# Retention attention, gated MoE and tanh MoE on one core: state products as four 64x64 tiles over two PSUM banks, block loads in two parts per batch on one queue

## The chip, the cores and the metric

The kernel runs on one core of one Trainium2 chip. The metric is device time in microseconds (us) of one execution; the time of a kernel is the median of several runs. The profile and the trace come from one further, profiled execution.

## The reference

Eight batches of eight heads with 576 positions of 64 numbers each go through retention attention; the result, 4608 tokens by 512, goes through a gated MoE and then a second MoE:

```python
scores = (q @ k.T) / sqrt(64)                      # per batch and head, 576 x 576
x   = (scores * gamma[h] ** (i - j) where i >= j, else 0) @ v
a, b = x @ w1, x @ w2                              # 512 -> 1024
y   = ((a * b) @ w3) @ w_out                       # 1024 -> 1024 -> 512
h   = y @ w2_in                                    # 512 -> 2048
out = (h - tanh(h)) @ w2_out                       # 2048 -> 512
```

## The kernel before, in words

**Dense products.** Every dense operand is split into a high and a low fp32r part, and `mm3` (L121, L122, L123) makes three matmuls of one product. Tokens go in 12 tiles of T = 384. The first stretch of the program is a loop over 96 **units**, a unit being one token tile and one of the eight 128-wide blocks of w1 and w2: `half_s` makes a = x w1 into one PSUM bank (psab), `finish` evicts the unit before (ScalarE copies a at L426, VectorE multiplies it by b out of the second bank at L428 into the tile pf), `half_s` makes b. The products pf leave for DRAM (pdr) on the queue of SyncE (SP) at the next unit's start: `later` holds the store, `tick` issues it (L116). The four banks of the pool psm serve psab and psw (the products of a fold w3 w_out, whose result w34 goes to DRAM and back, L510). After the units come the y product and the second MoE, which the change does not touch.

**Attention.** Each batch is taken in five chunks of 128 positions, the last of 64. A running state of 64x64 per head carries what earlier chunks leave. Per chunk: `attn_2` multiplies k and q of each head (pss, L263) and VectorE masks the result into pt (L265); `attn_3` makes the output pso from the state (L361, chunks after the first) and from pt and v (L367), and the state's increment psu (L375), which VectorE adds (L383 in a batch's first chunk, L385 after it); `attn_x` copies pso into the x tiles as high part (ScalarE, L398) and low part (VectorE, L399). Four more PSUM banks, the pool psa, are taken in turn by psq, psk, pss, pso and psu. The state is kept as one 128x128 block per pair of heads with zeros off the diagonal, so that a state product contracts over 128 rows and gives 64 columns.

**Two ways to do chunks.** The first two batches (10 chunks) are the **prologue**: written out by hand and then by the tables `chunk_at` and `conv_at`, with transposes of q and k on TensorE (L246), while the weights w1 and w2 are loaded and split (`Conv`, L137 to L167, mostly VectorE). The other six batches (**main part**) follow the list `stages`, one chunk each 2.26 units: q and k arrive in 32x32-blocked form (`load_qk` queues up small DMAs, 32 KB each; `trickle`, L299, issues up to TRK = 12 of them at a unit's start, in turn on SP's queue and on ScalarE's), GpSimd scales q (L328), VectorE transposes the blocks (L346, L348). `side_s` does the fold in small steps, at each unit's end; its last step loads w34 back (L510).

The order on each engine is the order in which the program is written. A DMA issue takes its place in the order of the engine that issues it, and all DMAs share eight semaphores in turn.

Of the kernel before, what the change touches and what calls it, by code (L numbers as in the profile page):

```python
# [8 lines left out]
F32 = mybir.dt.float32  # L9
# [4 lines left out]
AF = mybir.ActivationFunctionType  # L14
ALU = mybir.AluOpType
# [13 lines left out]
def retention_glu_tanh_kernel(  # L29
# [16 lines left out]
    PE, ACT, DVE, POOL, SP = nc.tensor, nc.scalar, nc.vector, nc.gpsimd, nc.sync  # L46
# [3 lines left out]
    P = 128  # L50
# [74 lines left out]
    class Conv:  # L125
# [5 lines left out]
        def load(self):  # L131
            self.pool, bufs = (hv, 4) if self.pool == "head" else (cv, 3)
            self.raw = self.pool.tile([P, 512], I64, name="raw", bufs=bufs)
            dst = self.raw
            if len(self.src.shape) == 3:
                dst = dst.rearrange("p (k m) -> p k m", k=self.src.shape[1])
            SP.dma_start(out=dst, in_=self.src)  # L137
# [65 lines left out]
    qsrc = [t.rearrange("b h s d -> b s h d") for t in (q, k, v)]  # L203
    chunks = [(b, c) for b in range(B) for c in range(NA)]
    A = {}
    state = cpool.tile([P, NP, P], F32, name="state")
    POOL.memset(state, 0.0)
    xt = {}

    def xtile(t):  # L210
# [43 lines left out]
    def attn_2(i, pool):  # L254
        b, c = chunks[i]
        s0, n = CH[c]
        kn, vn, qT, kT = A[i]
        pt = pool.tile([P, NP, 2, C], F32, name="pt")
        pss = [psa.tile([P, NP, C], F32, tag="a", name="pss") for _ in range(2)]
        for j in range(NP):  # L260
            for e in range(2):
                r = D * e
                PE.matmul(pss[e][:n, j, :n], kT[r:r + D, j, :n], qT[r:r + D, j, :n], start=True, stop=True)  # L263
        for e in range(2):
            DVE.tensor_tensor(  # L265
                pt[:n, :, e, :n], pss[e][:n, :, :n],
                mask[:n, :n].unsqueeze(1).to_broadcast([n, NP, n]), op=ALU.mult,
            )
        A[i] = (kn, vn, qT, pt)


    QK = {}
    pend = []

    def load_qk(i):

        if i >= len(chunks) or i in QK:
            return
        b, c = chunks[i]
        s0 = CH[c][0]  # L280
        e0 = min(s0 + 2 * C, S)
        m = (e0 - s0) // W
        ts = []
        for nm, src in (("q", q), ("k", k)):
            t = ap_.tile([P, NP, 2 * C // W, W], F32, name=f"{nm}b", bufs=2)
            ts.append(t)
            for r in range(P // W):
                o = t[r * W:r * W + W, :, :m]
                s_ = src[b, r // 2::2, s0:e0, (r % 2) * W:(r % 2) * W + W]
                for j in range(NP):  # L290
                    pend.append((t, o[:, j], s_[j].rearrange("(j i) c -> i j c", i=W)))
        QK[i] = ts
        if c + 1 < NA:
            QK[i + 1] = ts

    def trickle(n):
        for e in range(min(n, len(pend))):
            _, o, i_ = pend.pop(0)
            (SP, ACT)[e % 2].dma_start(out=o, in_=i_)  # L299

    def need(tile_):
        while any(e[0] is tile_ for e in pend):
            trickle(1)
# [12 lines left out]
            ts.append(t)  # L316
        KV[i] = ts

    def next_pair(i):
        return len(chunks) if i >= len(chunks) else i + (2 if chunks[i][1] + 1 < NA else 1)  # L320

    def stage_q(i):
        b, c = chunks[i]
        s0, n = CH[c]
        m, j0, k0 = n // W, s0 // W, (c % 2) * (C // W)
        need(QK[i][0])
        qn = QK[i][0][:, :, k0:k0 + m, :]
        POOL.tensor_tensor(  # L328
            qn, qn, dec_b[:, :, j0:j0 + m].unsqueeze(3).to_broadcast([P, NP, m, W]), op=ALU.mult
        )  # L330
# [7 lines left out]
    def stage_0(i):  # L338
        b, c = chunks[i]
        s0, n = CH[c]  # L340
        m, j0, k0 = n // W, s0 // W, (c % 2) * (C // W)
        qb, kb = QK.pop(i)
        need(kb)
        qn = qb[:, :, k0:k0 + m, :]
        kt = ap_.tile([P, NP, C // W, W], F32, name="kT")
        DVE.transpose(kt[:, :, :m, :], kb[:, :, k0:k0 + m, :])  # L346
        qt = ap_.tile([P, NP, C // W, W], F32, name="qT")
        DVE.transpose(qt[:, :, :m, :], qn)  # L348
        if c % 2 == 1 or c + 1 == NA:
            load_qk(next_pair(next_pair(i - c % 2)))  # L350
        A[i] = (*KV[i], qt.rearrange("p g j c -> p g (j c)"), kt.rearrange("p g j c -> p g (j c)"))

    def attn_3(i):
        b, c = chunks[i]
        s0, n = CH[c]
        kn, vn, qT, pt = A.pop(i)
        po = psa.tile([P, NP, C], F32, tag="a", name="pso")
        if c > 0:
            for j in range(NP):
                for e in range(2):  # L360
                    PE.matmul(  # L361
                        po[D * e:D * e + D, j, :n], state[:, j, D * e:D * e + D], qT[:, j, :n],
                        start=(j == 0), stop=False, skip_group_check=True,
                    )
        for j in range(NP):
            for e in range(2):
                PE.matmul(  # L367
                    po[D * e:D * e + D, j, :n], vn[:n, 2 * j + e, :], pt[:n, j, e, :n],
                    start=(c == 0 and j == 0), stop=(j == NP - 1), skip_group_check=True,
                )  # L370
        if c + 1 < NA:
            pu = psa.tile([P, NP, D], F32, tag="a", name="psu")
            for j in range(NP):
                for e in range(2):
                    PE.matmul(  # L375
                        pu[D * e:D * e + D, j, :], kn[:n, 2 * j + e, :], vn[:n, 2 * j + e, :],
                        start=True, stop=True,
                    )
            for e in range(2):
                sl = slice(D * e, D * e + D)  # L380
                st = state[sl, :, sl]
                if c == 0:
                    DVE.tensor_copy(st, pu[sl])  # L383
                else:
                    DVE.tensor_tensor(st, pu[sl], st, op=ALU.add)  # L385
        A[i] = po

    def attn_x(i):
        b, c = chunks[i]
        s0, n = CH[c]  # L390
        po = A.pop(i)
        t0 = b * S + s0
        while t0 < b * S + s0 + n:
            ti = t0 // T
            m = min((ti + 1) * T, b * S + s0 + n) - t0
            x = xtile(ti)
            a0, o0 = t0 - b * S - s0, t0 - ti * T
            ACT.activation(x[:, 0, :, o0:o0 + m], po[:, :, a0:a0 + m], AF.Copy)  # L398
            DVE.tensor_tensor(  # L399
                x[:, 1, :, o0:o0 + m], po[:, :, a0:a0 + m], x[:, 0, :, o0:o0 + m].bitcast(F32), op=ALU.subtract  # L400
            )
            t0 += m


# [15 lines left out]
    def finish():  # L420

        if not open_:
            return
        t, m, pss = open_.pop()
        a = tp.tile([P, T], F32, name="a", bufs=1)
        ACT.activation(a, pss[0][:, :T], AF.Copy)  # L426
        pf = tp.tile([P, T], F32, name="pf", bufs=3)
        DVE.tensor_tensor(pf, a, pss[1][:, :T], op=ALU.mult)  # L428
        later(SP, pdr[t][:, m], pf, 1)
        if m == FF - 1:  # L430
            del xt[t]


    def w12_target(m, i):
        def f(j):
            if i == 0:
                ws[m] = slot(m, f"w12_{m}")
            j.high = ws[m][:, i * 1024:i * 1024 + 512]
            j.low = ws[m][:, i * 1024 + 512:i * 1024 + 1024]
        return f  # L440

    q12 = Queue([
        Conv((w1, w2)[i][:, m * P:m * P + P].rearrange("(k p) c -> p k c", p=P), target=w12_target(m, i), pool="head")
        for m in range(FF) for i in range(2)
    ], ahead=3)
    wo = {}
# [114 lines left out]
    NH = 2 * NA  # L561
    J = q12.jobs
    warm = cpool.tile([P, 1], F32, name="warm")
    ACT.activation(warm, state[:, 0, 0:1], AF.Copy)
    attn_load(0)
    attn_load(1)
    J[0].load()
# [61 lines left out]
        stages += [(p - 1, stage_q, (i,)), (p, stage_0, (i,)), (p + 1, stage_1, (i,)), (p + 2, attn_4, (i,))]  # L629
    stages.sort(key=lambda e: e[0])  # L630

    TRK = 12
    NO = 84
    side_n = {}
    sn = 0
# [6 lines left out]
    for n, (t, m) in enumerate(units):  # L642
# [8 lines left out]
        if n == NO:  # L651
# [3 lines left out]
            lp[0] = lp_.enter_context(tc.tile_pool(name="lp", bufs=2, side="right", reuse_waits="tile"))  # L655
            side, sn = side_o(), 0
        n0, n1, steps = (N0, NO - 1, 79) if n < NO else (NO, len(units) - 3, 18)
        tick()
        trickle(TRK)
        i = chunk_at.get(n)  # L660
# [26 lines left out]
            scale_v(4)  # L687
            scale_q(5)
        if n == 10:
            load_qk(NH)  # L690
            load_kv(NH)
        if n == 13:
            load_qk(next_pair(NH))
        if n == len(units) - 5:
            for e in range(3):
                p_load(e)
# [4 lines left out]
        while si < len(stages) and stages[si][0] <= n:  # L701
            stages[si][1](*stages[si][2])
            si += 1
        while side is not None and sn < (n - n0 + 1) * steps / (n1 - n0):
            sn += 1
            if next(side, 1) == 1:
                side = None
# [205 lines left out]
```

## Time and profile before

| | us |
|---|---|
| three runs, median (lowest to highest) | 1647.47 (1646.09 to 1649.54) |
| profiled execution, its own time | 1644.21 |
| its span, first to last instruction | 1642.4 |
| TensorE busy in the span | 1603.5 (98%) |
| VectorE, ScalarE, GpSimd busy | 1121.9, 871.4, 30.6 |

The profiled execution lies 3.3 us below the median of the runs. The units run from 27 us to 638 us, the prologue's chunks until 106 us, and those of the main part until 580 us.

### The profile page before, as it was taken

How to read it: one execution, taken by the hardware profiler on the slowest of the kernel's cores; microseconds unless marked ns; L12 is line 12 of the kernel's file. 1: busy time of each engine (PE TensorE's matmuls, PEld its weight loads, DVE VectorE, ACT ScalarE, POOL GpSimd, SP SyncE). 2: the span in 40 equal slices, each digit the busy share in tenths (PEclk: the TensorE clock that was granted, in tenths of full speed). 3: DMA queues.
4: the chain of work that ended last, by engine and by line, in shares of the span. 5: the costliest groups of instructions: out<-in, count | busy, mean ns of one | idle time of the engine just before them, and what ended most of it. 6: DMA issues, size and time to landing. Idle time of an engine off the chain costs nothing.

```text
span 1642.4 us, 26856 instructions
## 1 busy us (share of the span) xinstructions
PE 1603.5 (98%) x10128; PEld 1492.8 (91%) x10128; DVE 1121.9 (68%) x2006; ACT 871.4 (53%) x1930; POOL 30.6 (2%) x35
## 2 busy tenths in 40 slices
PE   7899899999998999999999999999999999999999
PEld 6899889999898999999999999999999999999998
DVE  6964665455543357666658778778787877877876
ACT  5533333222322223444367777677767777777766
POOL 0000101010100000000000000000000000000000
PEclk9999999999999999999999999999999999999999
DMA  9646757465547257766540010001000000001000
GB/s 230 165 100 147 151 141 160 123 144 129 118 107 202 65 178 259 225 200 209 193 161 20 20 39 20 20 20 39 20 20 20 26 33 20 20 20 40 1 20 20
DMA packets 261250, 157.96 MB, mean 96 GB/s; under 512 B 209152, under 2 KB 238080, under 8 KB 261120
## 3 DMA queue, kind: packets, MB, share of 16 engines
q1 hardware_dynamic: 199488, 139.71, 30.3%
q10 hardware_dynamic: 61632, 16.53, 4.3%
q8 instruction: 79, 1.29, 0.3%
q14 instruction: 51, 0.42, 0.1%
HBM read 110.05 MB, written 46.14 MB: 95 GB/s over the span
## 4 chain that ended last, share of the span: by engine, by line
PE 86%; DMA 6%; DVE 5%; SPq 1%; ACT 1%; ACTq 1%; issue 1%; DVEq 0%
PE psh L123 8%; PE psh L122 8%; PE psh L121 8%; PE psout L122 8%; PE psout L121 8%; PE psout L123 8%; PE psab L121 6%; PE psab L123 6%; PE psab L122 6%; PE psy L121 4%; PE psy L123 4%; PE psy L122 4%; DMA pdr<-pf 2%; DMA qb<-in_q_dram 2%; PE pso L367 1%; DMA kb<-in_k_dram 1%
## 5 line engine op out<-in xcount | busy, mean ns | idle before, releaser
L121 PE MATMUL psab<-x,w 128*128 128x384 f32 x768 | 265.4, 346 | 15.3 <-ACT a L426 15.2
L123 PE MATMUL psh<-yhl,w2i 128*128 128x384 f32 x768 | 258.9, 337 | 0.0
L123 PE MATMUL psab<-x,w 128*128 128x384 f32 x768 | 258.5, 337 | 0.3 <-DVE x L399 0.3
L122 PE MATMUL psab<-x,w 128*128 128x384 f32 x768 | 258.4, 336 | 0.0
L121 PE MATMUL psh<-yhl,w2i 128*128 128x384 f32 x768 | 258.4, 336 | 0.0
L122 PE MATMUL psh<-yhl,w2i 128*128 128x384 f32 x768 | 258.3, 336 | 0.0
L122 PE MATMUL psout<-w2o,g 128*128 128x512 f32 x576 | 226.8, 394 | 0.0
L121 PE MATMUL psout<-w2o,g 128*128 128x512 f32 x576 | 225.9, 392 | 0.0
L123 PE MATMUL psout<-w2o,g 128*128 128x512 f32 x576 | 225.5, 391 | 0.0
L802 ACT ACTIVATE u<-psh 128x384 f32<-128x384 f32 x192 | 94.5, 492 | 221.5 <-PE psh L123 221.2
L121 PEld LDWEIGHTS psab<-x,w 128*128 128x128 f32 x768 | 145.3, 189 | 21.6 <-ACT a L426 17.9
L810 DVE TENSOR_TENSOR w<-u,psh 128x384 f32<-128x384 f32 x192 | 106.1, 553 | 80.8 <-ACT th L804 80.6
L823 DVE TENSOR_TENSOR g<-w,g 128x384 fp32r<-128x384 f32 x192 | 107.1, 558 | 69.1 <-ACT g L822 69.0
L121 PEld LDWEIGHTS psh<-yhl,w2i 128*128 128x128 f32 x768 | 144.2, 188 | 8.0
L122 PEld LDWEIGHTS psh<-yhl,w2i 128*128 128x128 f32 x768 | 144.1, 188 | 7.4
L426 ACT ACTIVATE a<-psab 128x384 f32<-128x384 f32 x96 | 46.8, 487 | 190.5 <-DMA qb<-in_q_dram 85.7
L123 PEld LDWEIGHTS psab<-x,w 128*128 128x128 f32 x768 | 145.3, 189 | 0.6 <-DVE x L399 0.6
L122 PEld LDWEIGHTS psab<-x,w 128*128 128x128 f32 x768 | 145.4, 189 | 0.3
L123 PEld LDWEIGHTS psh<-yhl,w2i 128*128 128x128 f32 x768 | 144.0, 187 | 0.0
L817 DVE COPY_PREDICATED w<-u,th 128x384 f32<-128x384 int32 x192 | 116.5, 607 | 20.9 <-DVE w L816 0.9
L123 PEld LDWEIGHTS psout<-w2o,g 128*128 128x128 f32 x576 | 108.3, 188 | 24.0
L121 PE MATMUL psy<-p,w 128*128 128x384 f32 x384 | 128.3, 334 | 0.0
(86 smaller groups left out, 2832.6 us busy)
## 6 DMA issues: line engine op xcount, KB each, us to landing
pdr<-pf SPq DMA_DIRECT2D x96, 192.0 KB, 3.0
pin<-pdr SPq DMA_DIRECT2D x48, 384.0 KB, 4.2
raw<-in_moe_w_dram SPq DMA_DIRECT2D x32, 512.0 KB, 4.7
raw<-in_moe_w_out_dram SPq DMA_DIRECT2D x24, 512.0 KB, 4.4
ydr<-ys ACTq DMA_DIRECT2D x12, 768.0 KB, 5.7
yin<-ydr SPq DMA_DIRECT2D x12, 768.0 KB, 4.3
out_dram<-os SPq DMA_DIRECT2D x36, 256.0 KB, 2.2
kn<-in_k_dram SPq DMA_DIRECT2D x32, 256.0 KB, 3.6
```

Source lines behind the costliest of these rows:

```text
L121: PE.matmul(ps, lh, rh, start=first, stop=False)
L122: PE.matmul(ps, ll, rh, start=False, stop=False)
L123: PE.matmul(ps, lh, rl, start=False, stop=last)
L367: PE.matmul(po[D * e:D * e + D, j, :n], vn[:n, 2 * j + e, :], pt[:n, j, e, :n], start=(c == 0 and j == 0), stop=(j == NP - 1), skip_group_ ...
L426: ACT.activation(a, pss[0][:, :T], AF.Copy)
L802: ACT.activation(u, h, AF.Square)
L810: DVE.tensor_tensor(w, u, h, op=ALU.mult)
L817: DVE.copy_predicated(w, u.bitcast(I32), th)
L823: DVE.tensor_tensor(g[:, 1, :], w, g[:, 0, :].bitcast(F32), op=ALU.subtract)
```

## The change

1. **State products.** The state is kept as 64x64 blocks, head e of a pair in rows 64e. pso becomes two PSUM banks, one for each e, and the four products of two pairs lie in four 64x64 quarters of the array. The products of pt and v keep their 128x64 shape; in a last chunk two GpSimd memsets zero the unused 64 rows of pt and v. The x tiles hold heads k and k+4 side by side in place of 2k and 2k+1, so each raw load of w1 and w2 becomes two DMAs of 64 partitions.
2. **VectorE and ScalarE.** The state update is one operation of 128x256 in place of two of 64x256. The copies to x become two operations on each engine, one per bank, in place of one of twice the size.
3. **Block loads.** q and k of a batch come in two parts (256 and 320 positions; one buffer for each), as 64 DMAs in place of 96, all on SP's queue, 8 at a unit's start. ScalarE issues none of them (before: half).
4. **finish.** The tile a is gone: ScalarE writes pf, VectorE multiplies in place, and pf has 2 buffers in place of 3.
5. **Side steps** run at a unit's start in place of its end.

```diff
-    state = cpool.tile([P, NP, P], F32, name="state")
-    POOL.memset(state, 0.0)
+    state = cpool.tile([P, NP, D], F32, name="state")
...
-            t = ap_.tile([P, NP, 2 * C // W, W], F32, name=f"{nm}b", bufs=2)
+            t = ap_.tile([P, NP, (e0 - s0) // W, W], F32, name=f"{nm}b{g}")
...
     def trickle(n):
-        for e in range(min(n, len(pend))):
+        for _ in range(min(n, len(pend))):
             _, o, i_ = pend.pop(0)
-            (SP, ACT)[e % 2].dma_start(out=o, in_=i_)
+            SP.dma_start(out=o, in_=i_)
...
-        po = psa.tile([P, NP, C], F32, tag="a", name="pso")
+        po = [psa.tile([P, NP // 2, C], F32, tag="a", name="pso") for _ in range(2)]
+        order = [(jj, e, hf) for jj in range(NP // 2) for e in range(2) for hf in range(2)]
         if c > 0:
-            for j in range(NP):
-                for e in range(2):
-                    PE.matmul(
-                        po[D * e:D * e + D, j, :n], state[:, j, D * e:D * e + D], qT[:, j, :n],
-                        start=(j == 0), stop=False, skip_group_check=True,
-                    )
+            for jj, hf, e in order:
+                r, o = slice(D * e, D * e + D), slice(D * hf, D * hf + D)
+                j = 2 * hf + jj
                 PE.matmul(
+                    po[e][o, jj, :n], state[r, j, :], qT[r, j, :n],
+                    start=(jj == 0), stop=False, skip_group_check=True,
                 )
...
-            for e in range(2):
-                sl = slice(D * e, D * e + D)
-                st = state[sl, :, sl]
-                if c == 0:
-                    DVE.tensor_copy(st, pu[sl])
-                else:
-                    DVE.tensor_tensor(st, pu[sl], st, op=ALU.add)
+            if c == 0:
+                DVE.tensor_copy(state, pu)
+            else:
+                DVE.tensor_tensor(state, pu, state, op=ALU.add)
...
+            for e in range(2):
+                xe, pe = x[:, :, e::2, o0:o0 + m], po[e][:, :, a0:a0 + m]
+                ACT.activation(xe[:, 0], pe, AF.Copy)
+                DVE.tensor_tensor(xe[:, 1], pe, xe[:, 0].bitcast(F32), op=ALU.subtract)
...
-        a = tp.tile([P, T], F32, name="a", bufs=1)
-        ACT.activation(a, pss[0][:, :T], AF.Copy)
-        pf = tp.tile([P, T], F32, name="pf", bufs=3)
-        DVE.tensor_tensor(pf, a, pss[1][:, :T], op=ALU.mult)
+        pf = tp.tile([P, T], F32, name="pf")
+        ACT.activation(pf, pss[0][:, :T], AF.Copy)
+        DVE.tensor_tensor(pf, pf, pss[1][:, :T], op=ALU.mult)
         later(SP, pdr[t][:, m], pf, 1)
...
-    TRK = 12
+    TRK = 8
```

What stands on ScalarE in the main part, around three units, before. L426 is finish's copy out of psab, L217 the scaling of v, L143 and L160 a step of the fold, L398 the copy to x, L299 a group of block loads.

```order
L299 DMA qb<-in_q_dram 32x8x32 x6
L426 ACTIVATE a<-psab 128x384
L217 ACTIVATE vn<-vn,dec 128x64 x8
L143 ACTIVATE cf<-raw 128x512
L160 ACTIVATE wo_1616<-cf 128x512
L299 DMA qb<-in_q_dram 32x8x32 x2
L299 DMA kb<-in_k_dram 32x8x32 x4
L426 ACTIVATE a<-psab 128x384
L398 ACTIVATE x<-pso 128x4x128
```

The same stretch with the change (L400 is the copy to x, L221 the scaling of v, L147 and L164 the fold):

```order
L426 ACTIVATE pf<-psab 128x384
L221 ACTIVATE vn<-vn,dec 128x64 x8
L426 ACTIVATE pf<-psab 128x384
L400 ACTIVATE x<-pso 128x2x128 x2
L147 ACTIVATE cf<-raw 128x512
L164 ACTIVATE wo_1630<-cf 128x512
```

No DMA issue stands ahead of a copy out of psab any more, and the copy to x is two. On SP, the issues of about two units of the main part before (L116 the store of pf, L315 the loads of k and v, L137 a weight's raw load):

```order
L299 DMA qb<-in_q_dram 32x8x32 x6
L315 DMA kn<-in_k_dram 128x8x64
L315 DMA vn<-in_v_dram 128x8x64
L137 DMA raw<-in_moe_w_out_dram 128x512
L116 DMA pdr_71<-pf 128x384
L299 DMA qb<-in_q_dram 32x8x32 x2
L299 DMA kb<-in_k_dram 32x8x32 x4
```

With the change (L301 the block loads, L317 k and v, L141 the raw load):

```order
L301 DMA qb_2203<-in_q_dram 32x10x32 x8
L317 DMA kn<-in_k_dram 128x8x64
L317 DMA vn<-in_v_dram 128x8x64
L116 DMA pdr_71<-pf 128x384
L301 DMA qb_2203<-in_q_dram 32x10x32 x8
L141 DMA raw<-in_moe_w_out_dram 128x512
```

SP issues eight blocks at a unit's start behind that unit's store, where it issued six. On TensorE in the prologue, chunk 5 (the first of the second batch, without a state product), before, with what each instruction waits for (Activation is ScalarE):

```order
L367 MATMUL pso<-pt,vn 64x128 x6
L375 MATMUL psu<-vn,kn 64x64 [waits PE_49]
L375 MATMUL psu<-vn,kn 64x64 x7
L263 MATMUL pss<-qT,kT 128x128 [waits Activation_49]
L263 MATMUL pss<-qT,kT 128x128 [waits PE_49]
L263 MATMUL pss<-qT,kT 128x128 x6
```

With the change:

```order
L370 MATMUL pso<-pt,vn 64x128 x5
L378 MATMUL psu<-vn,kn 64x64 [waits Activation_49]
L378 MATMUL psu<-vn,kn 64x64 x7
L267 MATMUL pss<-qT,kT 128x128 [waits Activation_49]
L267 MATMUL pss<-qT,kT 128x128 [waits DVE_49]
L267 MATMUL pss<-qT,kT 128x128 x6
```

pso takes two of psa's four banks and psu a third, so the second bank of the next pss is psu's own: it now waits for VectorE's state update, which reads psu.

## Rows read from the trace of the kernel before

**Rows 1.** Busy time of each engine in three stretches, with TensorE's granted clock.

```profile
0.00:82.00 82.00, 65.35 (x665) 58.97 (x667) 65.01 (x117) 46.84 (x128) 0.73 (x5) 0.98 0.85 198
82.00:580.00 498.00, 479.29 (x3949) 447.48 (x3946) 258.38 (x469) 149.15 (x427) 29.84 (x30) 0.99 0.55 131
580.00:1642.40 1062.40, 1058.89 (x5520) 986.31 (x5519) 798.49 (x1420) 675.38 (x1376) 0.00 (x0) 1.00 0.22 72
```

**Rows 2.** Waits by waiting line and releaser: total us, times, longest.

```profile
ACT a L426 <- DMA qb<-in_q_dram: 85.7, 19, 10.1
ACT a L426 <- DMA kb<-in_k_dram: 57.5, 20, 5.3
PE psab L121 <- ACT a L426: 15.2, 13, 5.4
PE psw L121 <- ACT a L426: 3.4, 3, 1.8
```

**Rows 3.** Timeline, ScalarE, 508 to 537 us: start, us, instruction, idle before it.

```profile
514.14 0.47 ACT L426 ACTIVATE a<-psab 128x384 f32<-128x384 f32 x1
...
526.24 4.89 ACTq L299 DMA_DIRECT2D qb<-in_q_dram  x6
531.18 0.49 ACT L426 ACTIVATE a<-psab 128x384 f32<-128x384 f32 x1 [10.12 <-DMA qb<-in_q_dram]
```

**Rows 4.** Busy time around that place, as in rows 1; the clock follows GpSimd's column.

```profile
531.70:536.40 4.70, 4.67 (x15) 4.68 (x16) 1.77 (x4) 2.37 (x9) 0.06 (x1) 0.50 0.80 169
```

**Rows 5.** Timeline, SP's queue, 505 to 532 us.

```profile
509.42 10.17 SPq L510 DMA_DIRECT2D w<-wd  x8
519.68 1.08 SPq L116 DMA_DIRECT2D pdr<-pf  x1
...
526.84 3.86 SPq L299 DMA_DIRECT2D qb<-in_q_dram  x6
```

**Rows 6.** DMA issues: count, KB each, median us from issue to landing.

```profile
pdr<-pf SPq DMA_DIRECT2D x96, 192.0 KB, 3.0
```

**Rows 7.** Single lines: count, ns least/median/most of one, first and last start.

```profile
L426 ACT ACTIVATE a<-psab x96: 462/490/495, 40.5 to 636.2; 128x384 f32<-128x384 f32 x96
...
L299 SPq DMA_DIRECT2D kb<-in_k_dram x136: 311/431/1344, 126.7 to 539.0; - x136
```

**Rows 8.** Timeline, TensorE, one chunk of the main part.

```profile
376.24 1.09 PE L361 MATMUL pso<-qT,state 128*64 128x128 f32 x16
377.17 1.04 PE L367 MATMUL pso<-pt,vn 128*64 128x128 f32 x16
378.04 0.64 PE L375 MATMUL psu<-vn,kn 128*64 128x64 f32 x16
378.61 0.66 PE L467 MATMUL pst<-cst,w3f 128*128 128x128 f32 x4
```

**Rows 9.** Timeline, TensorE, a last chunk of 64 positions.

```profile
44.39 0.69 PE L361 MATMUL pso<-qT,state 128*64 128x64 f32 x16
45.01 0.68 PE L367 MATMUL pso<-pt,vn 64*64 64x64 f32 x16
45.62 1.16 PE L263 MATMUL pss<-qT,kT 64*128 64x128 f32 x16
```

**Rows 10.** Timeline of all engines in the prologue, chunk 5.

```profile
55.28 1.16 PE L263 MATMUL pss<-qT,kT 64*128 64x128 f32 x16
...
60.21 0.85 DVE L383 COPY state<-psu 64x256 f32<-64x256 f32 x2
...
61.21 0.63 PE L246 MATMUL psq<-cst,qn 128*128 128x128 f32 x4 [2.46 <-DVE state L383]
```

**Rows 11.** Timeline of TensorE and VectorE in the prologue, the chunk after.

```profile
68.47 1.16 PE L263 MATMUL pss<-qT,kT 64*128 64x128 f32 x16
...
71.13 0.85 DVE L385 TENSOR_TENSOR state<-psu,state 64x256 f32<-64x256 f32 x2
72.01 0.42 DVE L399 TENSOR_TENSOR x<-pso,x 128x256 fp32r<-128x256 f32 x1
```

More of the change, by code (lines that the diff above doesn't have):

```diff
@@ L134, in load @@
             dst = self.raw
+            if isinstance(self.src, tuple):
+                for o, src in zip((0, D), self.src):
+                    SP.dma_start(out=dst[o:o + D].rearrange("p (k m) -> p k m", k=KD), in_=src)
+                return
             if len(self.src.shape) == 3:
@@ L268, in attn_2 @@
             )
+        if n < P:
+            POOL.memset(pt[n:, :, :, :n], 0.0)
+            POOL.memset(vn[n:], 0.0)
         A[i] = (kn, vn, qT, pt)
@@ L273, in retention_glu_tanh_kernel, with load_qk @@
     pend = []
-    def load_qk(i):
-        if i >= len(chunks) or i in QK:
+    def load_qk(b, g):
+        if b >= B:
             return
[L279 to L282, printed above, removed]
+        s0, e0 = ((0, 2 * C), (2 * C, S))[g]
         ts = []
         for nm, src in (("q", q), ("k", k)):
-            t = ap_.tile([P, NP, 2 * C // W, W], F32, name=f"{nm}b", bufs=2)
+            t = ap_.tile([P, NP, (e0 - s0) // W, W], F32, name=f"{nm}b{g}")
             ts.append(t)
             for r in range(P // W):
-                o = t[r * W:r * W + W, :, :m]
                 s_ = src[b, r // 2::2, s0:e0, (r % 2) * W:(r % 2) * W + W]
                 for j in range(NP):
[L291 to L294, printed above, removed]
+                    pend.append((t, t[r * W:r * W + W, j], s_[j].rearrange("(j i) c -> i j c", i=W)))
+        QK[b, g] = ts
     def trickle(n):
-        for e in range(min(n, len(pend))):
+        for _ in range(min(n, len(pend))):
             _, o, i_ = pend.pop(0)
-            (SP, ACT)[e % 2].dma_start(out=o, in_=i_)
+            SP.dma_start(out=o, in_=i_)
     def need(tile_):
@@ L317, in load_kv @@
         KV[i] = ts
-    def next_pair(i):
-        return len(chunks) if i >= len(chunks) else i + (2 if chunks[i][1] + 1 < NA else 1)
     def stage_q(i):
@@ L324, in stage_q @@
         s0, n = CH[c]
-        m, j0, k0 = n // W, s0 // W, (c % 2) * (C // W)
-        need(QK[i][0])
-        qn = QK[i][0][:, :, k0:k0 + m, :]
+        g = int(c > 1)
+        m, j0, k0 = n // W, s0 // W, (c - 2 * g) * (C // W)
+        need(QK[b, g][0])
+        qn = QK[b, g][0][:, :, k0:k0 + m, :]
         POOL.tensor_tensor(
@@ L340, in stage_0 @@
         s0, n = CH[c]
-        m, j0, k0 = n // W, s0 // W, (c % 2) * (C // W)
-        qb, kb = QK.pop(i)
+        g = int(c > 1)
+        m, k0 = n // W, (c - 2 * g) * (C // W)
+        qb, kb = QK[b, g]
         need(kb)
@@ L348, in stage_0 @@
         DVE.transpose(qt[:, :, :m, :], qn)
-        if c % 2 == 1 or c + 1 == NA:
-            load_qk(next_pair(next_pair(i - c % 2)))
+        if c in (1, NA - 1):
+            load_qk(b + 1, g)
         A[i] = (*KV[i], qt.rearrange("p g j c -> p g (j c)"), kt.rearrange("p g j c -> p g (j c)"))
@@ L356, in attn_3 @@
         kn, vn, qT, pt = A.pop(i)
-        po = psa.tile([P, NP, C], F32, tag="a", name="pso")
+        po = [psa.tile([P, NP // 2, C], F32, tag="a", name="pso") for _ in range(2)]
+        order = [(jj, e, hf) for jj in range(NP // 2) for e in range(2) for hf in range(2)]
         if c > 0:
-            for j in range(NP):
-                for e in range(2):
-                    PE.matmul(
-                        po[D * e:D * e + D, j, :n], state[:, j, D * e:D * e + D], qT[:, j, :n],
-                        start=(j == 0), stop=False, skip_group_check=True,
-                    )
-        for j in range(NP):
-            for e in range(2):
+            for jj, hf, e in order:
+                r, o = slice(D * e, D * e + D), slice(D * hf, D * hf + D)
+                j = 2 * hf + jj
                 PE.matmul(
-                    po[D * e:D * e + D, j, :n], vn[:n, 2 * j + e, :], pt[:n, j, e, :n],
-                    start=(c == 0 and j == 0), stop=(j == NP - 1), skip_group_check=True,
-                )
+                    po[e][o, jj, :n], state[r, j, :], qT[r, j, :n],
+                    start=(jj == 0), stop=False, skip_group_check=True,
+                )
+        for jj, e, hf in order:
+            o, j = slice(D * hf, D * hf + D), 2 * hf + jj
+            PE.matmul(
+                po[e][o, jj, :n], vn[:, 2 * j + e, :], pt[:, j, e, :n],
+                start=(c == 0 and jj == 0), stop=(jj == 1), skip_group_check=True,
+            )
         if c + 1 < NA:
@@ L378, in attn_3 @@
                     )
-            for e in range(2):
-                sl = slice(D * e, D * e + D)
-                st = state[sl, :, sl]
-                if c == 0:
-                    DVE.tensor_copy(st, pu[sl])
-                else:
-                    DVE.tensor_tensor(st, pu[sl], st, op=ALU.add)
+            if c == 0:
+                DVE.tensor_copy(state, pu)
+            else:
+                DVE.tensor_tensor(state, pu, state, op=ALU.add)
         A[i] = po
@@ L397, in attn_x @@
             a0, o0 = t0 - b * S - s0, t0 - ti * T
[L398 to L401, printed above, removed]
+            for e in range(2):
+                xe, pe = x[:, :, e::2, o0:o0 + m], po[e][:, :, a0:a0 + m]
+                ACT.activation(xe[:, 0], pe, AF.Copy)
+                DVE.tensor_tensor(xe[:, 1], pe, xe[:, 0].bitcast(F32), op=ALU.subtract)
             t0 += m
@@ L440, in w12_target, with rows @@
         return f
+    def rows(w):
+        return tuple(w[o:o + DM // 2].rearrange("(k p) c -> p k c", p=D) for o in (0, DM // 2))
     q12 = Queue([
-        Conv((w1, w2)[i][:, m * P:m * P + P].rearrange("(k p) c -> p k c", p=P), target=w12_target(m, i), pool="head")
+        Conv(rows((w1, w2)[i][:, m * P:m * P + P]), target=w12_target(m, i), pool="head")
         for m in range(FF) for i in range(2)
@@ L563, in retention_glu_tanh_kernel @@
     warm = cpool.tile([P, 1], F32, name="warm")
-    ACT.activation(warm, state[:, 0, 0:1], AF.Copy)
+    POOL.memset(warm, 0.0)
+    ACT.activation(warm, warm, AF.Copy)
     attn_load(0)
@@ L657, in retention_glu_tanh_kernel @@
         n0, n1, steps = (N0, NO - 1, 79) if n < NO else (NO, len(units) - 3, 18)
+        while side is not None and sn < (n - n0 + 1) * steps / (n1 - n0):
+            sn += 1
+            if next(side, 1) == 1:
+                side = None
         tick()
@@ L689, in retention_glu_tanh_kernel @@
         if n == 10:
-            load_qk(NH)
+            load_qk(2, 0)
             load_kv(NH)
         if n == 13:
-            load_qk(next_pair(NH))
+            load_qk(2, 1)
         if n == len(units) - 5:
@@ L703, in retention_glu_tanh_kernel @@
             si += 1
[L704 to L707, printed above, removed]
     assert si == len(stages) and not pend and len(held) < 2 and len(w34) == FF, (si, len(pend), held)
```

## The prediction

> **What bounds the kernel now.** I read the stages first. From 580 us on, TensorE is busy in 1058.9 of 1062.4 us, and the change touches nothing there. From 82 to 580 us it is busy in 479.3 of 498.0: 18.7 us are idle. Before 82 us it is busy in only 65.4 of 82.0, and VectorE in 65.0 [rows 1]. So there are three things to move: 18.7 us of stalls in the middle, TensorE's own work there, and the head, where TensorE and VectorE wait for each other.
>
> The table of waits names the 18.7: TensorE waits for ScalarE's copy out of psab, 15.2 us at psab and 3.4 at psw, together 18.6. And the copy itself waited for DMA issues of q's and k's blocks, 85.7 and 57.5 us in 39 cases [rows 2]. The timeline shows how: the six block issues that stand ahead of a copy on ScalarE took 4.89 us, and the copy began only at 531.18, after 10.12 us without work [rows 3]; TensorE's longest wait of 5.4 us [rows 2] ends there. [...]
>
> **Part 1: no DMA issues on ScalarE.** The 16 waits of 18.6 us lose their releaser. I treat the longest apart. The other 15 are 18.6 − 5.4 = 13.2 us; I take 12 of them as gone, since ScalarE has little else in the main part (149 us of 498 busy [rows 1]) and a copy may still come late here and there. Bounds: −13.2, and −9 if a third of them comes back through the later parts. Each split copy to x adds one ScalarE operation, estimated at no more than a whole copy out of psab, 0.47 us [rows 3], in a unit of (636.2 − 40.5)/95 = 6.3 us [rows 7]; ScalarE's idle time covers it, and without that cover a copy out of psab would be half a microsecond late, still inside the slack of the two psab pairs.
>
> **Part 2: pf's two buffers, and the place at 510 to 531 us.** ScalarE's copy now writes pf, so it must wait until the store of two units earlier has landed. In most units that store is issued within a unit and lands 3.0 us later [rows 6], well before. One place bites: SP issues the eight loads of w34 for 10.17 us, and the store behind them starts only at 519.68 [rows 5]; it lands at about 522.7. The copy that now starts at 514.14 [rows 3] is two units behind the tile of that store, as I count the units there; it would end near 523.2. TensorE wants that bank again a unit later, at 514.1 + 6.3 = 520.4. That is an estimated stall of 2.8 us, and with some half clock behind it 3.5. In place of the old event, 5.4 + 2.35 = 7.8 us, this leaves a gain of 4; bounds 0 (the same loss at a new place) and −7.8. That side steps come one unit earlier moves the loads with the stores around them; I price it at nothing, since both queue up in the same order, and its cover is this bound.
>
> **Part 3: the products.** Sixteen records of a state product over 128 columns take 377.17 − 376.24 = 0.93 us from start to start, those of pt and v 0.87, i.e. eight steps of 0.109 us, two halves of the array side by side [rows 8]. In quarters of 64x64, four of them side by side make four steps, 0.44 us: a gain of 0.44 in each of 24 chunks (three of 128 rows with a state in eight batches). In the last chunks, with half of the columns, half of that: 0.22 in 8 chunks. Against this stands a change of tile shape: the products of a last chunk, 128x64 then 64x64 tiles, go 0.62 and 0.61 us from start to start [rows 9], each with a change of shape, where half of the 0.87 for twice the columns would be 0.44. That is 0.17 or 0.18 for a change at most; I take 0.15, since some of it may be a fixed part of the shorter products. The 24 chunks get one more (64x64 to 128x64, between the state's product and pt's); the last chunks had one already. Sum: −24 × 0.44 − 8 × 0.22 + 24 × 0.15 = −8.7 us; three quarters of it, −6.5, in the main part, where TensorE bounds. No row shows four quarters at once; the pairs of rows 8 lie in columns, and pss shows pairs in rows, sixteen records in 1.16 us [rows 9]. Bounds of the main part: +2.7 (no further overlap, the change of shape paid 18 times) and −9.2 (no price for the shape).
>
> [...]
>
> **Part 4: the prologue.** pso takes two of four banks, and pss's second bank is psu's, free only after the state update. At chunk 5 pss starts at 55.28 and the update ends at 61.06, because VectorE is about 5 us behind there, with matmuls done in between until 58.75 and then an idle 2.46 [rows 10]. Those matmuls now come after the update: one operation of 128x256 in place of two saves 0.43, so pss goes on at 60.6, ends near 61.6, and the 2.4 us of matmuls between 56.4 and 58.8 (pss's end and the idle time's start) follow until 64.0; psq starts at 64.0 and not at 61.21, +2.8, of which I give back 0.7 for a shorter VectorE queue and quicker products: +2.1. At the next such place pss starts at 68.47 and the update ends at 71.98 [rows 11]; TensorE is 2.1 late by then, so 3.5 − 2.1 = 1.4 of wait, of which the shorter update and products give back 0.2: +1.2. At the other five places of this kind I take nothing, and −0.3 from what is left of the products' gain of 2.2: +3 in all. Bounds: −2 (the gain comes through, VectorE sheds its lag) and +7 (both waits in full and a third like them). VectorE's copy to x is two operations, 0.42 us for each half [rows 11]; it eats part of the 0.43 that a state update saves, and is inside the 0.7 above.
>
> **Part 5: SP.** SP issues 64 blocks per batch where it issued 48, some 95 DMAs with stores, k, v and raw loads. The median of one block (k's; q's are like it) is 0.43 us [rows 7], and for the larger DMAs I take the same, so 41 us of the 5 × 2.26 × 6.3 = 71 us that a batch lasts. Hidden behind the units; price nothing. What is queued behind: pf's store stands ahead of the blocks of its unit, so a late block makes the next store late, which is part 2's bound. The 16 extra DMAs of the raw loads and GpSimd's memsets (two in a last chunk, and the products of pt and v wait for them) lie in units with idle SP and GpSimd; nothing.
>
> **Sum**, against the profiled 1644.2: −12 − 4 − 6.5 + 3 = −19.5; I take −19. The profiled execution is 3.3 us below the median, so I forecast 1647.5 − 19 = **1628 us** as median.
>
> **Rivals.** (a) *Likeliest*, 1622 to 1635. (b) *Everything clears*: stalls −13.2, the event −6, products −7, prologue neutral: −26, 1621. For it: ScalarE is free, and pf's late store is an estimate. Against it: VectorE's lag in rows 10 is real. (c) *Quarters don't overlap or the array empties at each change of shape*: part 3 turns to +2.7, the rest −12 − 4 + 3: −10, 1637. For it: no row shows four at once. (d) *The change doesn't do what it says*: the copies wait as long as before, now for pf's store behind eight blocks on SP, and the prologue takes what the products give: 1647. For it: stores with 3.0 us to landing and block bursts on one queue; against: the copy has two units' time. (e) *Slower: SP becomes the bound*. A batch's 95 issues need 71 us at 0.75 us each; the median is 0.43, six in a burst took 3.86/6 = 0.64 [rows 5], a single one up to 1.34 [rows 7]. At 0.78 a batch lasts 74 in place of 71 us, 6 × 3.1 = +19: 1666. It decides from 0.75 us on.
>
> **How the numbers follow.** Chances: (a) 0.50, (b) 0.20, (c) 0.12, (d) 0.07, (e) 0.11. About 0.2%, 3.3 us, is what a measurement of this kernel can tell from no change. (a), (b) and (c) are faster: 0.82; (d) the same, 0.07; (e) slower, 0.11. A range from 1614 (bounds: −13.2 − 7.8 − 9.2 − 2 = −32, 1615) to 1642 ((c) with the prologue at +7: −6, 1641) holds these three.
>
> **What would show it.** Right: no DMA issue ahead of a copy out of psab, and TensorE idle under 6 us from 82 to 580 us; state products about 0.45 us per group, and 0.15 between; in the prologue a wait of pss for the state update of about 5 us at chunk 5; one wait of a copy for pf's store right behind the loads of w34. Wrong: block issues on SP of 0.7 us and more with q's scaling waiting for them; state products that keep 0.9 us per group; TensorE's idle time before 82 us up by more than 7.

## The result, and the profile after

The changed kernel takes 1633.2 us (median of four runs, 1631.02 to 1635.63), the kernel before 1647.68 beside it: a ratio of 0.9912, 95% interval 0.9893 to 0.9931, or −14.5 us. 1628 was forecast, 5 us less, in a range of 1614 to 1642. The profiled execution took 1632.1 us against 1644.2.

Busy time by stage, as in [rows 1], with the middle cut where the attention ends now:

```profile
0.00:82.00 82.00, 62.22 (x616) 55.42 (x617) 61.59 (x117) 46.64 (x135) 1.29 (x7) 0.94 1.01 189
82.00:567.80 485.80, 476.47 (x3997) 441.81 (x3996) 250.49 (x483) 151.50 (x466) 37.60 (x44) 1.00 0.57 136
567.80:1630.30 1062.50, 1058.54 (x5518) 985.96 (x5517) 798.45 (x1421) 674.93 (x1375) 0.00 (x0) 1.00 0.22 72
```

The middle stage is 12.2 us shorter, and TensorE is idle there for 9.3 us where it was 18.7. The head is worse: busy 62.2 of 82 where it was 65.4. The third row is as before. The waits, as in [rows 2]:

```profile
PE psab L121 <- ACT pf L426: 8.1, 5, 3.8
PE pss L267 <- DVE state L383: 6.3, 2, 4.0
...
PE pss L267 <- DVE state L385: 3.0, 4, 1.5
```

The copy out of psab no longer waits for a DMA issue; the wait that took its place is for a store of pf, 54.9 us in 21 cases. The longest of them (timeline, ScalarE, behind the loads of w34):

```profile
508.86 0.49 ACT L426 ACTIVATE pf<-psab 128x384 f32<-128x384 f32 x1 [8.28 <-DMA pdr<-pf]
```

and on SP's queue, which answers to [rows 5]:

```profile
493.01 4.73 SPq L513 DMA_DIRECT2D w<-wd  x8
498.05 0.32 SPq L116 DMA_DIRECT2D pdr<-pf  x1
```

The other four that reach TensorE, at 153, 226, 239 and 245 us, lie where SP issues one DMA after another. The one at 239 us: the product (VectorE) is ready at 226.41, its store is issued only at 232.36, behind the blocks, k, v and a raw load, and the copy that needs the buffer starts at 238.01.

```profile
225.85 0.56 DVE L427 TENSOR_TENSOR pf<-pf,psab 128x384 f32<-128x384 f32 x1 [1.86 <-ACT pf L426]
...
226.17 3.91 SPq L301 DMA_DIRECT2D kb<-in_k_dram  x8
...
232.36 0.38 SPq L116 DMA_DIRECT2D pdr<-pf  x1
...
238.01 0.49 ACT L426 ACTIVATE pf<-psab 128x384 f32<-128x384 f32 x1 [5.00 <-DMA pdr<-pf]
```

A chunk of the main part on TensorE answers to [rows 8], and the start of a last chunk to [rows 9]:

```profile
391.20 0.67 PE L364 MATMUL pso<-qT,state 64*64 64x128 f32 x16
391.80 1.09 PE L370 MATMUL pso<-pt,vn 128*64 128x128 f32 x16
392.72 0.63 PE L378 MATMUL psu<-vn,kn 128*64 128x64 f32 x16
...
499.11 0.46 PE L364 MATMUL pso<-qT,state 64*64 64x64 f32 x16
499.50 0.69 PE L370 MATMUL pso<-pt,vn 128*64 128x64 f32 x16
```

The state's products go 0.60 us from start to start where they went 0.93, those of pt 0.92 where they went 0.87; in the last chunk the state's go 0.39, where they went 0.62. All chunks of the main part agree with these within 0.01 or 0.02 us, before and after. So more of the state's products run at once than before: sixteen take 0.60 us for 0.93, while the record of one lasts 269 ns (median of L364) for 272 (L361 before). That four run at a time is the prediction's reading; no row shows the number.

One row serves from here on as a mark of where the prologue ends: the sixteenth copy out of psab (timeline, ScalarE). Before:

```profile
128.94 0.49 ACT L426 ACTIVATE a<-psab 128x384 f32<-128x384 f32 x1 [1.76 <-PE psab L123]
```

After:

```profile
134.13 0.49 ACT L426 ACTIVATE pf<-psab 128x384 f32<-128x384 f32 x1 [1.77 <-PE psab L123]
```

So the prologue lost 5.2 us in this execution. (The expectations below name the copies of units 8 and 12, which moved by 5.4 and 5.2.) The last copy starts at 624.0 where it started at 636.2 [rows 7]: from the mark on, the change gained 12.2 + 5.2 = 17.4.

### The profile page after: what moved, and what is told of

It reads as the page before. It is cut to its first block, busy times and chain, and to the rows that moved or that the text cites. A ratio compares the mean times of both kernels' runs of the same rounds, so it can differ in the third digit from the quotient of the medians.

```text
span 1630.3 us, 26792 instructions
## 1 busy us (share of the span) xinstructions
PE 1597.2 (98%) x10128; PEld 1483.2 (91%) x10128; DVE 1110.5 (68%) x2018; ACT 873.1 (54%) x1974; POOL 38.9 (2%) x51
## 4 chain that ended last, share of the span: by engine, by line
PE 92%; DMA 3%; DVE 2%; SPq 1%; ACT 1%; issue 1%; ACTq 0%; DVEq 0%
PE psh L123 8%; PE psh L122 8%; PE psh L121 8%; PE psout L122 8%; PE psout L121 8%; PE psout L123 8%; PE psab L121 8%; PE psab L123 7%; PE psab L122 7%; PE psy L122 4%; PE psy L121 4%; PE psy L123 4%; PE pss L267 2%; PE pso L370 2%; DMA pdr<-pf 1%; PE psw L121 1%
## 5 line engine op out<-in xcount | busy, mean ns | idle before, releaser
L121 PE MATMUL psy<-p,w 128*128 128x384 f32 x384 | 128.3, 334 | 0.0
L122 PE MATMUL psy<-p,w 128*128 128x384 f32 x384 | 128.3, 334 | 0.0
```

Of the source, the lines that this page charges most:

```text
L121: PE.matmul(ps, lh, rh, start=first, stop=False)
L122: PE.matmul(ps, ll, rh, start=False, stop=False)
```

## The experiments

Every ratio is against runs of the kernel before on the same chip; 0.001 is 1.65 us. Two questions led: why 8.1 us of waits remain in the middle, and what the prologue's 5.2 us are. Theory A was the prediction's: the in-place pf with two buffers, and pss's wait for psu's bank. Theory D came from the trace after: in the prologue ScalarE now waits for raw loads, where the kernel before has no such wait (L147 is the first step of converting one):

```profile
ACT cf L147 <- DMA raw<-in_moe_w_dram: 10.2, 5, 3.4
```

**Three buffers for pf** (`pf3`).

```diff
-        pf = tp.tile([P, T], F32, name="pf")
+        pf = tp.tile([P, T], F32, name="pf", bufs=3)
```

> The changed kernel with three buffers for pf in place of two; nothing else. Theory A (the 8.1 us that TensorE still waits for ScalarE's copy come from the copy's wait for the store of two units earlier, since pf is written in place in two buffers): the waits of the copy for a store, 54.9 us in 21 cases, all but vanish, TensorE's 8.1 us fall below 1.5, the half clock behind 509 us goes too, and the time falls by 8 to 10 us to about 1624. Rival B (the copy is late for another reason, SP's long burst of block issues above all, and the store is only the wait that ended last): the waits change their releaser, and the time falls by less than 3 us.

0.9882 (0.9865 to 0.9899), 1627.1 us: 5 us less than with two (give or take 4), not 8 to 10. TensorE's waits for the copy are gone, as A says, and those of the copy for a store fell from 54.9 us to 14.6. But a stall that the earlier ones had hidden came up, in TensorE's waits and, as its cause, on VectorE's timeline:

```profile
PE pss L267 <- DVE qT L349: 3.7, 1, 3.7
...
162.16 0.71 DVE L347 STREAM_TRANSPOSE kT<-kb 128x512 f32<-128x512 f32 x1 [5.46 <-DMA kb<-in_k_dram]
```

The third chunk of the main part's first batch waits for blocks that SP issues too late. TensorE stood idle 3.65 us, and the next 4.4 us had a granted clock of 0.61.

**Block loads and finish alone, on the kernel before** (`loads_pf_only`): the edits of load_qk, trickle, the stages' use of the two parts, finish, TRK = 8.

```diff
-            (SP, ACT)[e % 2].dma_start(out=o, in_=i_)
+            SP.dma_start(out=o, in_=i_)
...
+        pf = tp.tile([P, T], F32, name="pf")
```

> The kernel before with two parts of the change alone: block loads in two parts per batch on SP's queue, and finish in place with two pf buffers. Products, banks, x copies, and the place of the side steps as before. Theory A: the stalls behind ScalarE's DMA issues go (18.6 us, and 2.35 of half clock) and some 10 come back as waits for pf's store; the prologue is as before and does not pay the 5 us that the changed kernel pays there. About -11 us, 1636. Rival B (the loss in the prologue is of SP's queue or the raw loads and not of the banks): -6 or less.

0.9938 (0.9922 to 0.9955), −10 us, as A expects: the prologue is where it was (the marking copy within 0.1 us of before), and the copy's waits cost TensorE 7.8 us, the longest of 3.7 us again behind the loads of w34.

**Products alone, on the kernel before** (`products_only`): the edits of the state, pso, the state update, x and the raw loads.

```diff
-        po = psa.tile([P, NP, C], F32, tag="a", name="pso")
+        po = [psa.tile([P, NP // 2, C], F32, tag="a", name="pso") for _ in range(2)]
...
+                for o, src in zip((0, D), self.src):
+                    SP.dma_start(out=dst[o:o + D].rearrange("p (k m) -> p k m", k=KD), in_=src)
```

> The kernel before with the other parts alone: state products as four 64x64 quarters over two banks, one state update, split x copies, raw loads in two DMAs. Block loads, finish and side steps as before. Theory A: -6.3 us from the products in the main part, +5 in the prologue by pss's wait for the state update, and a stall or two of ScalarE more or less: about -1 us (-4 to +2), 1646. Rival C (TensorE's gain in the main part is given back at the next wait, since ScalarE's DMA issues end later than TensorE there anyway): +3 or more.

0.9973 (0.9963 to 0.9983), −4.4 us: just below the range given. −10.2 and −4.4 add up to −14.6, against the −14.5 of the whole. Neither of the two kernels moves the side steps, so the sum leaves nothing for them, within the some 4 us that the three intervals allow.

**The prologue with one bank and products as before** (`prologue_one_bank`), main part as changed:

```diff
+        pro = i < 2 * NA
+        if pro:
+            pb = psa.tile([P, 2, NP // 2, C], F32, tag="a", name="pso")
+            po = [pb[:, 0], pb[:, 1]]
...
+                    PE.matmul(
+                        po[e][o, jj, :n], stp[:, j, r], qT[:, j, :n],
```

> The changed kernel, but in the prologue the state is kept in blocks of 128x128 with zeros as before, its products go in 128x64 tiles, pso is one bank, and the state update is two operations; the main part is as changed. Theory A (the prologue's +5.2 us come from pss's wait for the state update on psu's bank): TensorE's waits of pss for the state update, 9.3 us, fall below 2, the copy of unit 12 starts 4 to 6 us earlier, and the time falls by 3 to 6 us to about 1629; the products' gain there, 2.2, is given up. Rival D (the prologue is late because of the raw loads in two halves or the split copies to x): less than 1.5 us.

0.9943 (0.9927 to 0.9958), 1637.6 us: slower than the changed kernel. pss waits for no state update any more, yet the marking copy starts at 133.62, 0.5 us earlier. The waits moved to q's scaling and to a stage further on (TensorE's waits):

```profile
PE psq L252 <- DVE qn L237: 10.4, 3, 5.7
...
PE pss L269 <- ACT kT L256: 3.0, 2, 2.3
```

This kernel also gives VectorE back the second state operation and lets the two copies to x wait for each other, so it doesn't clear the bank alone; but A's 3 to 6 us did not come. Its profiled execution is 2.1 us slower than the changed kernel's, as much as the products' gain that it gives up there (2.2, an estimate); why the medians lie 5 us apart is open.

**psu taken out by ScalarE in the prologue** (`state_by_act`).

```diff
+            if i < 2 * NA:
+                su = state if c == 0 else sap.tile([P, NP, D], F32, name="su")
+                ACT.activation(su, pu, AF.Copy)
+                if c > 0:
+                    POOL.tensor_tensor(state, su, state, op=ALU.add)
```

> The changed kernel, but in the prologue ScalarE copies psu out of its bank (into the state in a batch's first chunk) and GpSimd adds it to the state in the others, so that pss no longer waits for VectorE's queue. Theory A: pss's waits for the state update, 9.3 us, fall below 4, and the time falls by 3 to 5 us to about 1629. Theory D: the waits go but TensorE then waits for k, v and weights that are loaded late: within 1.5 us of the changed kernel.

0.9913 (0.9893 to 0.9933), the changed kernel's 0.9912. pss's waits for the bank are 6.0 us where they were 9.3, and the marking copy is 1.6 us earlier (132.56), which the time does not show. So 3.3 us less of waiting is worth at most 1.6 at the mark; the 6.0 us that are left this run does not test.

**Raw loads in two halves, alone, on the kernel before** (`raw_two_64`, `raw_two_128`). The first:

```diff
+            if self.pool is hv:
+                for o in (0, D):
+                    SP.dma_start(out=dst[o:o + D].rearrange("p (k m) -> p k m", k=KD), in_=self.src[o:o + D])
+                return
```

The second has the same number of DMAs with all 128 partitions in each:

```diff
+                dk = dst.rearrange("p (k m) -> p k m", k=KD)
+                for o in (0, 2):
+                    SP.dma_start(out=dk[:, o:o + 2], in_=self.src[:, o:o + 2])
```

> The kernel before, with each raw load of w1 and w2 made as two DMAs of 64 partitions, as in the changed kernel; nothing else. Theory D (the prologue is late by about 5 us because of the 16 extra DMAs on SP's queue, which is busy from the start to 60 us, each issue waiting until a DMA eight before it has landed: the loads of k, v and weights come later and later): the copy of unit 8 starts 3 to 6 us later than before, and the time rises by 3 to 6 us. Theory A (it is pss's wait for the state update on psu's bank): no change, within 1 us.

> The kernel before, with each raw load of w1 and w2 as two DMAs of all 128 partitions and half of the columns; nothing else. It tells two forms of theory D apart. D1 (the number of DMAs counts, since only eight are under way at a time and half loads carry fewer bytes each): as late as with two halves of 64 partitions, +3 to +6 us. D2 (64 partitions are slow, since the bytes go to half of the partitions): under half of that loss. Theory A: no change.

The marking copy, with halves of 64 partitions:

```profile
134.10 0.49 ACT L430 ACTIVATE a<-psab 128x384 f32<-128x384 f32 x1 [1.76 <-PE psab L123]
```

and with halves of the columns:

```profile
129.78 0.49 ACT L431 ACTIVATE a<-psab 128x384 f32<-128x384 f32 x1 [1.76 <-PE psab L123]
```

134.10 is the changed kernel's 134.13, with none of its banks. Each is one execution, but the others agree: in all eight kernels here with halves of 64 partitions on SP's queue the marking copy starts between 132.6 and 136.3, in the three without between 128.9 and 129.8. ScalarE's waits for raw loads, which the kernel before doesn't have, with halves of 64 partitions and with halves of the columns:

```profile
ACT cf L147 <- DMA raw<-in_moe_w_dram: 12.7, 5, 3.9
```

```profile
ACT cf L148 <- DMA raw<-in_moe_w_dram: 1.9, 1, 1.9
```

Busy time from 12 to 24 us, when loads follow one another, ends with the GB/s moved: the kernel before, halves of 64 partitions, halves of the columns, and the changed kernel:

```profile
12.00:24.00 12.00, 9.01 (x134) 8.05 (x135) 10.41 (x20) 8.38 (x25) 0.00 (x0) 1.00 1.23 267
```

```profile
12.00:24.00 12.00, 8.12 (x99) 7.23 (x99) 9.09 (x17) 8.34 (x24) 0.00 (x0) 0.86 1.23 208
```

```profile
12.00:24.00 12.00, 10.23 (x123) 9.13 (x122) 9.77 (x19) 8.79 (x25) 0.00 (x0) 0.86 1.21 266
```

```profile
12.00:24.00 12.00, 8.46 (x123) 6.85 (x121) 8.81 (x17) 8.53 (x27) 0.00 (x0) 1.00 1.25 212
```

The DMA engines are as busy in all four (a share of 1.21 to 1.25), but with 64 partitions they move 208 to 212 GB/s in place of 267: at the mark and in the rate it is D2 and not D1, though here only a part of the traffic is in halves. A raw load lands 6.2 us after its issue (median until 110 us) where a half of the columns takes 4.2, and the loads of k beside it 7.4 for 5.0. So halves of 64 partitions are slower; why, no run shows. In the medians the loss hardly shows, where 3 to 6 us were expected, and they don't tell the two kernels apart: 1.0008 (0.9998 to 1.0019) for 64, 1.0002 (0.9992 to 1.0012) for 128. The profiled execution of the first was its slowest, 1653.3 us against a median of 1647.4. So the 5.2 us at the mark are shown, and what of them the end of that kernel keeps is open, between −0.3 and +3.1 us.

**Twelve blocks per unit at first** (`pf3_trickle12`), on three buffers.

```diff
-        trickle(TRK)
+        trickle(TRK if n > 18 else 12)
```

> The changed kernel with three pf buffers, and until unit 18 up to 12 block loads at a unit's start in place of 8. With three buffers alone TensorE still lost 3.65 us at 160 us, where a transpose waited for blocks of the main part's first batch, and then ran some microseconds at half clock. Theory A2 (that stall is the 8 per unit: the first two parts need eight units): the stall goes, and the time is 3 to 5 us under the 1627 of three buffers, about 1623. Rival (SP's queue is full there anyway, and more blocks per unit only make the burst longer): within 1 us of 1627.

0.9892 (0.9877 to 0.9906): the rival. The stall at 160 us is gone, and another of 4.6 us stands at 149 (timeline, ScalarE):

```profile
152.94 0.68 ACT L147 ACTIVATE cf<-raw 128x512 f32<-128x512 f32 x1 [8.89 <-DMA raw<-in_moe_w_out_dram]
153.51 0.48 ACT L426 ACTIVATE pf<-psab 128x384 f32<-128x384 f32 x1
```

The raw loads of w_out came behind the longer bursts on SP, the fold's first step waited for them on ScalarE, and the copy out of psab behind that. (The next expectation names pf's store as the cause of that stall; this row says that it was the raw load.)

**The first batch's blocks earlier** (`pf3_early`), on three buffers.

```diff
         if n == 10:
-            load_qk(2, 0)
             load_kv(NH)
-        if n == 13:
+        if n == 7:
+            load_qk(2, 0)
             load_qk(2, 1)
```

> The changed kernel with three pf buffers, and the two parts of the main part's first batch asked for at unit 7 in place of units 10 and 13, eight blocks at a unit's start as changed: these blocks then go out from 95 to 145 us, ahead of the raw loads of w_out and the loads of k and v. With three buffers alone TensorE stood 3.65 us at 160 us for them, and with twelve per unit 4.6 us at 149 us for pf's store behind them. Theory A3 (what TensorE loses between 140 and 170 us is SP's crowd of that place): no stall over 1 us there, 4 to 6 us under the 1627 of three buffers, about 1622. Rival: another wait takes the place (within 1.5 us of 1627).

0.9861 (0.9846 to 0.9877), 1622.8 us: as expected, the fastest of all, by the ratios 8 us under the changed kernel. Against three buffers alone the ratios give 3.5 us, with intervals that overlap a little; the profiled executions lie 4.3 us apart. The middle is full (busy time by stage):

```profile
82.00:565.00 483.00, 482.61 (x4047) 448.74 (x4046) 254.04 (x490) 152.68 (x470) 37.62 (x44) 1.00 0.58 141
```

**Second halves of the raw loads on GpSimd's queue** (`pf3_raw_pool`; with the earlier blocks `pf3_early_pool`; with psu by ScalarE too `pf3_early_pool_act`).

```diff
-                for o, src in zip((0, D), self.src):
-                    SP.dma_start(out=dst[o:o + D].rearrange("p (k m) -> p k m", k=KD), in_=src)
+                for eng, o, src in zip((SP, POOL), (0, D), self.src):
+                    eng.dma_start(out=dst[o:o + D].rearrange("p (k m) -> p k m", k=KD), in_=src)
```

> The changed kernel with three pf buffers, and the second half of each raw load of w1 and w2 on GpSimd's queue in place of SP's. Two halves of 128 partitions left the prologue of the kernel before as it was (unit 8 at +0.84 us), two of 64 made it late (+5.2 in the profiled execution). Theory D2 (a load of 64 partitions moves its bytes more slowly, and SP's queue does them one behind the other): with both halves under way at once the prologue's loss of 5.4 us shrinks to 2 or less, and the time is 3 to 4 us under the 1627 of three buffers. Theory A (pss's wait on psu's bank): within 1 us of 1627, and the copy of unit 8 as late as before.

> Both of the two kernels beside it at once: three pf buffers, first batch's blocks asked for at unit 7, second halves of the raw loads on GpSimd's queue. If both causes stand and are apart, their gains add: about 1618. If either falls, the time is that of the other.

> As the kernel with both, and psu taken out of its bank by ScalarE in the prologue (GpSimd adds it to the state), as in an earlier run, where the prologue was 1.6 us shorter but the time was the changed kernel's. If the wait on psu's bank is a cause of its own beside the raw loads, it gives 2 to 4 us more, about 1615; if it only stands where TensorE would wait for late loads, nothing (within 1 us of the kernel with both).

0.9932 (0.992 to 0.9945), 0.9901 (0.9887 to 0.9914) and 0.9887 (0.9873 to 0.99): the first two some 8 and 7 us worse than the same kernels without. GpSimd has nothing ahead of these loads, so they no longer stand behind q, k and v of the first chunks, and q came late: in the second of these kernels VectorE's two waits for its loads come to 14.9 us, the longest of 8.1, where they are 7.9 and 5.1 in the changed kernel. TensorE's first product (timeline), which starts at 5.81 us in the changed kernel:

```profile
9.12 1.12 PE L250 MATMUL psq<-cst,qn 128*128 128x128 f32 x4 [9.12 <-DVE qn L235]
```

The order of the loads changed with the queue, so this says nothing on whether two halves at once would do; a raw load of the new layout in one DMA of 128 partitions was not tried. psu by ScalarE takes the 1629.05 to 1627.14, less than the 2 to 4 us of a cause of its own, with intervals that overlap: undecided.

## Why the prediction was right, and where its terms were off

**The stalls behind ScalarE's DMA issues** (−12 for 15 of them). They went, all of them, as the waits after show. But the term has a counterpart that was priced at one place alone: four waits for pf's store outside the w34 place cost 8.1 − 3.8 = 4.3 us, and 1.2 had been left for anything. "In most units that store is issued within a unit and lands 3.0 us later, well before" is the step that failed in size: 21 copies waited 54.9 us for a store, five of them long enough for TensorE. In the four cases the store was issued 6.0 to 8.6 us after its product was ready and took 4.6 to 5.6 us to land. Three buffers gave these waits back. So the changed kernel missed the sign of being right that was given for this stage: TensorE is idle for 9.3 us there, not under 6.

**The place behind w34's loads** (−4 of 7.8). The mechanism was right to the instruction: the copy behind those loads waits for the store of two units earlier. It cost 3.8 us of idle time where 2.8 were estimated, and a lower clock behind it: from 509.4 to 513.0 the granted clock was 0.69, so an estimated 3.6 × 0.31 = 1.1 us more; the place gave 7.8 − 4.9 = 2.9 and not 4. The store's issue was earlier than before (498.05), but eight loads of 512 KB lay ahead of it in the queue, the last of which landed at 508.3, and the store itself at 508.8, 10.7 us after its issue, where the median of 3.0 had been taken. The 2.35 us of clock in the 7.8 no run shows as such: it is half of the 4.70 us of [rows 4], an estimate from their granted clock of 0.50; matmuls of 384 columns started every 0.32 us there, and every 0.17 to 0.19 behind it.

**The products** (−6.5 in the main part). 0.33 us less per chunk on the state, 0.05 more on pt's products, 0.28 net, 18 times, and 0.23 in six last chunks: −6.4. If four steps take the prediction's 0.44, a change of shape costs 0.16 us in front of pt's products (0.60 against 0.44) and about 0.05 behind, 0.2 together where 0.15 was taken; no run has quarters without a change of shape, so 0.16 is an estimate. At that price it did not eat the gain; whether the array empties at such a change, as rival (c) has it, no run shows.

**The prologue** (+3). The size was 5.2; that it lies inside the bounds is luck, since they were worked out from another reason. pss does wait 4.0 us at chunk 5 for the state update, as forecast, and 9.3 in all; yet two kernels in which it waits not at all or less moved the mark by 0.5 and 1.6 us. "The 16 extra DMAs of the raw loads [...] lie in units with idle SP and GpSimd; nothing" is the step that failed: SP is issuing for 48.7 of the first 60 us before and for 55.9 with the change, and with halves of 64 partitions the rate from 12 to 24 us fell from 267 to 212 GB/s. Raw loads in such halves, alone, put the mark where the whole change puts it. What the wait on psu's bank costs beside them, and what the quicker products give back there, is not parted, and no run shows how much of the 5.2 us the loads cost at the end of the changed kernel.

**SP as the bound** did not come true as a rival: the median of a block is 0.45 us after (0.43 before), and the main part ended 12 us earlier. But "hidden behind the units; price nothing" was wrong in part. From 131 to 242 us, where the main part starts, issues fill 90 of SP's 111 us, and the four late stores above come from there: they stand behind the blocks and loads of the unit before, which is the wait that rival (d) names. And SP's order at that place was worth some 3.5 us more (0.9882 against 0.9861), which was not seen ahead.

Sum: stalls in the middle −17.4 + 6.4 = −11.0 in the profiled execution, where −16 was forecast; prologue +5.2 for +3; together 7 us. The median shows 5 of them. The profiled executions of the two kernels lie 12.1 us apart and the medians 14.5, and that difference is no merit of the sum.

## What to carry to other kernels

A wait that is removed shows the one that lay under it: three buffers for pf gave 5 us of the 8 expected until the block loads of the next place were moved, and then some 3.5 more. When a buffer is given up to make room, price every release that it now waits for and not only the worst one. A load split by partitions is not the same load: same bytes, same number of DMAs, and 208 against 266 GB/s from 12 to 24 us.

## What the hardware showed that I had not expected

A product of four 64x64 quarters gave 0.60 us for sixteen matmuls of 128 columns against 0.93 in halves, the price of the change of shape included. With raw loads in halves of 64 partitions all traffic from 12 to 24 us came to 208 to 212 GB/s, with the DMA engines as busy (a share of 1.23 and 1.25) as at 267 (1.23). And a store behind eight loads of 512 KB on its queue took 10.7 us to land, over three times the median of its kind, 3.2 us.
